# Pairing two tokens per partition, transposing them as one 32-bit element, and giving GpSimd half of an elementwise product

## The chip, the cores and the metric

The kernel runs on one NeuronCore of one Trainium2 chip. The metric is device time in microseconds (us); a figure for a kernel is the median of its runs. In this text PE is the TensorE matrix engine, PEld its weight loads, DVE the VectorE, ACT the ScalarE and POOL the GpSimd.

A program on one core still scatters: the kernel before ran between 224.1 and 230.8 us in all rounds of this study. Each comparison is therefore made with runs of the kernel before on the same chip in the same rounds. The record calls a run slow when it is more than 1.5% above the fastest run of the same kernel in those rounds, and the others fast. The medians here include slow runs, the ratios leave them out.

## The reference, cut to what matters

```python
def _attn_ref(x, f_logit, lower_bound):            # x, f_logit: (4, 6336, 256)
    sig = 1.0 / (1.0 + np.exp(-f_logit))
    f = lower_bound + (1.0 - lower_bound) * sig
    i = 1.0 - f
    for t in range(S):
        h = f[:, t] * h + i[:, t] * x[:, t]         # a scan over the tokens
        y[:, t] = h

def _moe_ref(x, w_h, w_t, b_t):                    # on the 25344 tokens of y
    H = np.maximum(x @ w_h, 0.0)
    T = 1.0 / (1.0 + np.exp(-(x @ w_t + b_t)))
    return T * H + (1.0 - T) * x
```

A recurrence over the tokens is followed by a small gated layer on each token.

## The kernel before

The tokens are cut into units of 1024 (a few are smaller, at the start and at the end). Tokens arrive on partitions, eight to a partition, and the scan runs along the free dimension (128x1024 in the profile), so PE transposes two intermediate values: `u` (the gate) and `bv` (gate times input).

```python
    def load(n, name, src):                        # token j*128 + p on partition p
        ...
            pin(nc.sync.dma_start(t[:, :nb], src[b, a:a + nb * P, :].rearrange("(j p) d -> p j d", p=P)))
    def gate(n):                                   # ACT: u = sigmoid(-f_logit), 16 bits
        ...
        pin(nc.scalar.activation(u[:np_, :nb], st[n]["lt"][:np_, :nb], AF.Sigmoid, scale=-1.0))
    def product(n, after):                         # POOL: bv = u * x, two tokens at a time
        ...
            ins = pin(nc.gpsimd.tensor_mul(bv[:np_, q:q + 2], st[n]["u"][:np_, q:q + 2], st[n]["xt"][:np_, q:q + 2]))
    def decay_pe(n, m):                            # PE: eight 16-bit transposes; b_pe does the same with bv
        ...
                pin(nc.tensor.transpose(uT[:, c + j * np_:c + (j + 1) * np_], st[n]["u"][:np_, j, h * P:(h + 1) * P],
                                        ident_h[:np_, :np_]))
```

After the transposes, ACT makes `f` from `uT`, and DVE scans (`y`). PE multiplies `y` with two weights (`gp`, `zp`), ACT makes `t` of `zp`, and DVE makes `d` of `gp`. The product `e = d * t` is shared: GpSimd takes the last `SHARE` of the 1024 columns, and it does so after DVE's part.

```python
    SHARE = 256

    def e_dve(n):
        N = width(n)
        e = ffn.tile([P, NH, NB * P], BF16, tag="e", name="e")
        ...
        ins = pin(nc.vector.tensor_mul(e[:, :, :M], d[:, :, :M], t[:, :, :M]))
        if M < N:
            follow(pin(nc.gpsimd.tensor_mul(e[:, :, M:N], d[:, :, M:N], t[:, :, M:N])), ins)
```

PE turns the result back to tokens in two halves. `o_pe(n, 0)` reads columns 0 to 511 of `e`, `o_pe(n, 1)` reads columns 512 to 1023, each with 8 matmuls on `y` and 8 on `e`, alternating; ACT copies the result `op` out as `o`.

```python
    def o_pe(n, q):
        ...
            for h in range(NH):
                o = op[:np_, j - j0, h * P:(h + 1) * P]
                pin(nc.tensor.matmul(o, st[n]["y"][:, h, cols], diag[:, h], start=True, stop=False))
                pin(nc.tensor.matmul(o, st[n]["e"][:, h, cols], ident_b, start=False, stop=True))
```

Of the kernel before, what the change touches and what calls it, by code (L numbers as in the profile page):

```python
# [11 lines left out]
FP32 = mybir.dt.float32  # L12
BF16 = mybir.dt.bfloat16
FP16 = mybir.dt.float16
AF = mybir.ActivationFunctionType
# [4 lines left out]
def kernel(  # L20
# [16 lines left out]
    nc = tc.nc  # L37
    B, S, D = x.shape
    assert D == 256
    P = 128  # L40
    NH = D // P
    NB = 8
# [5 lines left out]
    units = []  # L48
# [4 lines left out]
    for s0 in range(rest, S, NB * P):  # L53
        for b in range(B):
            last = s0 + NB * P == S and b == B - 1
            a = s0
# [5 lines left out]
    singles = ctx.enter_context(tc.tile_pool(name="singles", bufs=1))  # L62
    inp = ctx.enter_context(tc.tile_pool(name="inp", bufs=5))
    upool = ctx.enter_context(tc.tile_pool(name="upool", bufs=3))
    mid = ctx.enter_context(tc.tile_pool(name="mid", bufs=2))
# [5 lines left out]
    st = [dict() for _ in range(NU)]  # L71

    def pin(ins):
        return tc.keep_in_program_order(ins)

    def load(n, name, src):
        np_, nb, _, b, a = units[n]
        t = inp.tile([P, NB, D], FP32, tag=name, name=name)
        if isinstance(b, int):
            pin(nc.sync.dma_start(t[:, :nb], src[b, a:a + nb * P, :].rearrange("(j p) d -> p j d", p=P)))  # L80
        else:
            t4 = t[:np_, :nb].rearrange("p (b j) d -> p b j d", j=2)
            for j in range(2):
                pin(nc.sync.dma_start(t4[:, :, j], src[b, a + j * np_:a + (j + 1) * np_, :].rearrange("b p d -> p b d")))
        st[n][name] = t

    def store(n, j0, j1):
# [19 lines left out]
    for n in range(2):  # L107
        load(n, "lt", f_logit)
        load(n, "xt", x)

    ident_b = singles.tile([P, P], BF16, name="ident_b")
    make_identity(nc, ident_b)
    ident_h = singles.tile([P, P], FP16, name="ident_h")
    make_identity(nc, ident_h)

# [23 lines left out]

    def gate(n):  # L140
        np_, nb = units[n][:2]
        u = upool.tile([P, NB, D], FP16, tag="u")
        pin(nc.scalar.activation(u[:np_, :nb], st[n]["lt"][:np_, :nb], AF.Sigmoid, scale=-1.0))  # L143
        st[n]["u"] = u

    def follow(ins, after):

        if after is not None:
            tc.add_manual_dep(ins.ins, after.ins.name, mybir.DependencyInfo(
                mybir.DependencyClass.Sync, mybir.DependencyReason.DATA), reason="shared port")  # L150

    def product(n, after):
        np_, nb = units[n][:2]
        bv = mid.tile([P, NB, D], BF16, tag="bv")
        for q in range(0, nb, 2):
            ins = pin(nc.gpsimd.tensor_mul(bv[:np_, q:q + 2], st[n]["u"][:np_, q:q + 2], st[n]["xt"][:np_, q:q + 2]))  # L156
            if q == 0:
                follow(ins, after)
        st[n]["bv"] = bv

    def width(n):
        return units[n][0] * units[n][1]

    def both(n, m, key, make):


        if width(n) > 512:
            st[n][key, m] = make()
            yield st[n][key, m], m, 0
        elif m == 0:  # L170
            st[n][key, 0] = st[n][key, 1] = t = make()
            for k in range(NH):
                yield t, k, k * 512

    def col(n, m):
        return 0 if width(n) > 512 else m * 512

    def decay_pe(n, m):
        np_, nb = units[n][:2]
        for uT, h, c in both(n, m, "uT", lambda: ps1.tile([P, NB * P], FP16, tag="uT", name="uT")):  # L180
            for j in range(nb):
                pin(nc.tensor.transpose(uT[:, c + j * np_:c + (j + 1) * np_], st[n]["u"][:np_, j, h * P:(h + 1) * P],  # L182
                                        ident_h[:np_, :np_]))

    def decay_act(n, h):
        N, c = width(n), col(n, h)
# [3 lines left out]
                                 scale=ncc[:, h:h + 1], bias=1.0))  # L190

    def b_pe(n, m):
        np_, nb = units[n][:2]
        for bT, h, c in both(n, m, "bT", lambda: ps1.tile([P, NB * P], BF16, tag="bT", name="bT")):
            for j in range(nb):
                pin(nc.tensor.transpose(bT[:, c + j * np_:c + (j + 1) * np_], st[n]["bv"][:np_, j, h * P:(h + 1) * P],  # L196
                                        ident_b[:np_, :np_]))

    carry = {}

# [36 lines left out]
        pin(nc.vector.scalar_tensor_tensor(st[n]["d"][:, m, :N], st[n]["y"][:, m, :N], ncc[:, m:m + 1],  # L237
                                           st[n]["gp", m][:, c:c + N], op0=ALU.mult, op1=ALU.max))

    SHARE = 256  # L240

    def e_dve(n):

# [2 lines left out]
        st[n]["e"] = e  # L246
        M = N - SHARE if N == NB * P else N
        d, t = st[n]["d"], st[n]["t"]
# [33 lines left out]
    for n in range(-3, NU + 2):  # L282
        if ok(n + 4) and n + 4 > 1:
            load(n + 4, "lt", f_logit)
            load(n + 4, "xt", x)
        p, pp = n - 1, n - 2
# [11 lines left out]
        if ok(n + 1):  # L298
            decay_pe(n + 1, 0)
            decay_act(n + 1, 0)  # L300
        if ok(p):
            d_dve(p, 0)
        if ok(n):
            b_pe(n, 1)
# [10 lines left out]
        if ok(n + 2):  # L315
            gate(n + 2)
# [5 lines left out]
        if ok(n + 1):  # L322
            b_pe(n + 1, 0)
            decay_pe(n + 1, 1)
            decay_act(n + 1, 1)
# [4 lines left out]
        if ok(n + 2):  # L330
            product(n + 2, after)
# [32 lines left out]
```

## Time and profile before

| | kernel before |
|---|---|
| time, median of the first three runs | 226.26 us (226.25 to 229.24) |
| span of the profiled run | 226.9 us |
| start of POOL's first `e` of a full unit | 48.57 us |
| period of a unit (20 periods of POOL's `e`, 48.57 to 207.09) | 7.93 us |

The page's first part gives busy time and its share of the span:

```profile
PE 195.0 (86%) x2008; PEld 136.9 (60%) x2008; DVE 202.1 (89%) x159; ACT 199.1 (88%) x198; POOL 140.0 (62%) x131
```

Three engines stand close together, so a change that burdens one of them may change the bound.

The waits of the whole run (engine, line, what was waited for: us in total, times, longest) have few long ones:

```profile
DVE y L207 <- PE bT L196: 11.7, 5, 4.1
PE bT L196 <- DVE y L207: 8.3, 22, 2.5
```

DVE waited for PE's `bT` only five times, four of them before 44 us and one near the end (217.93 us), while PE waited for DVE 22 times. DVE sets the pace.

### The profile page before, as it was taken

Reading aid. Unit: us, or ns where it says so; the run is one execution under the profiler, and the core shown is the slowest. Engines: PE = TensorE matmul, PEld = TensorE weight load, DVE = VectorE, ACT = ScalarE, POOL = GpSimd, SP = SyncE. Lnnn points to the kernel's source line nnn. Section 1 sums busy time; section 2 is a strip of 40 time slices with the busy share of each in tenths; the row PEclk is TensorE's granted clock in tenths of the full one; section 3 lists DMA queues with packets and bytes.
Section 4 is the critical chain, followed back from the end, with each engine's and each line's share of the span. In section 5 each row is a group of like instructions: output and inputs, shape, how many; then the busy total and the mean of one; then the engine's idle time right before and its main releaser. Section 6 shows DMA issues by size and latency. Waiting matters only on the chain.

```text
span 226.9 us, 4999 instructions
## 1 busy us (share of the span) xinstructions
PE 195.0 (86%) x2008; PEld 136.9 (60%) x2008; DVE 202.1 (89%) x159; ACT 199.1 (88%) x198; POOL 140.0 (62%) x131
## 2 busy tenths in 40 slices
PE   0588495989999999999999999999999999998971
PEld 0356365656766666676666657666665766665661
DVE  1499657799999999999999999999999999999871
ACT  4459946799999999999999999999999999976873
POOL 2654870745966786696678669667866966764300
PEclk9999857899999999999999999999999999999998
DMA  6999999999999999999999999999999997542444
GB/s 179 307 386 386 383 390 390 390 390 387 399 385 385 399 394 389 384 397 382 382 391 395 388 390 402 395 384 403 396 387 397 396 349 276 202 185 95 185 185 185
DMA packets 60262, 78.69 MB, mean 347 GB/s; under 512 B 2384, under 2 KB 53584, under 8 KB 60240
## 3 DMA queue, kind: packets, MB, share of 16 engines
q1 hardware_dynamic: 59152, 77.86, 93.9%
q10 hardware_dynamic: 1088, 0.53, 0.9%
q8 instruction: 15, 0.25, 0.4%
q14 instruction: 7, 0.06, 0.1%
HBM read 52.43 MB, written 25.95 MB: 345 GB/s over the span
## 4 chain that ended last, share of the span: by engine, by line
DVE 52%; issue 23%; PE 13%; DMA 4%; ACT 3%; POOL 3%; DVEq 0%; SPq 0%; ACTq 0%; POOLq 0%
DVE y L207 25%; DVE d L237 19%; DVE e L249 8%; PE gp L218 4%; PE zp L218 3%; POOL bv L156 3%; DMA xt<-in_x_dram 2%; PE bT L196 2%; PE uT L182 2%; DMA lt<-in_f_logit_dram 1%; PE op L267 1%; PE op L268 1%; ACT o L276 1%; ACT u L143 1%; ACT t L231 1%
## 5 line engine op out<-in xcount | busy, mean ns | idle before, releaser
L156 POOL TENSOR_TENSOR bv<-u,xt 128x512 bf16<-128x512 f16 (+1 forms) x100 | 114.3, 1172 | 18.9 <-DMA xt<-in_x_dram 7.2
L207 DVE TENSOR_TENSOR_SCAN y<-f,y,bT 128x1024 bf16<-128x1024 f16 (+2 forms) x54 | 113.7, 2105 | 7.9 <-PE bT L196 7.6
L231 ACT ACTIVATE t<-zp,bt 128x1024 bf16<-128x1024 f32 (+3 forms) x58 | 56.9, 994 | 13.5 <-PE zp L218 13.5
L218 PEld LDWEIGHTS <-w_sb 128*128 128x128 f16 x408 | 39.7, 100 | 43.1 <-issue 10.0
L237 DVE SCALAR_TENSOR_TENSOR d<-y,ncc,gp 128x1024 bf16<-128x1024 bf16 (+3 forms) x58 | 63.8, 1101 | 1.0 <-PE gp L218 0.9
L189 ACT ACTIVATE f<-uT,ncc 128x1024 f16<-128x1024 f16 (+3 forms) x58 | 58.4, 1007 | 4.2 <-PE uT L182 4.2
L251 POOL TENSOR_TENSOR e<-d,t 128x512 bf16<-128x512 bf16 x22 | 25.5, 1159 | 56.3 <-PE gp L218 56.3
L218 PE MATMUL gp<-y,w_sb 128*128 128x512 bf16 (+2 forms) x204 | 53.3, 385 | 3.7 <-DVE d L237 1.3
L218 PE MATMUL zp<-y,w_sb 128*128 128x512 bf16 (+2 forms) x204 | 52.6, 382 | 0.1
L267 PE MATMUL op<-diag,y 128*128 128x128 f16 (+1 forms) x400 | 50.8, 221 | 2.2 <-ACT o L276 2.2
L276 ACT COPY o<-op 128x1024 f32<-128x1024 f32 (+2 forms) x51 | 50.9, 997 | 1.9 <-PE op L268 1.7
L143 ACT ACTIVATE u<-lt 128x2048 f16<-128x2048 f32 (+3 forms) x29 | 49.0, 1689 | 3.9 <-DMA lt<-in_f_logit_dram 3.9
L268 PE MATMUL op<-ident_b,e 128*128 128x128 bf16 (+1 forms) x400 | 50.8, 220 | 0.0
L268 PEld LDWEIGHTS <-e 128*128 128x128 bf16 (+1 forms) x400 | 44.9, 115 | 7.5 <-POOL bv L156 1.3
L267 PEld LDWEIGHTS <-y 128*128 128x128 bf16 (+1 forms) x400 | 45.0, 114 | 5.7 <-issue 0.3
L196 PE MATMUL bT<-ident_b,bv 128*128 128x128 bf16 (+1 forms) x400 | 32.8, 224 | 16.6 <-DVE y L207 8.3
L196 PEld LDWEIGHTS <-bv 128*128 128x128 bf16 (+1 forms) x400 | 26.9, 100 | 23.8 <-issue 15.2
L182 PE MATMUL uT<-ident_h,u 128*128 128x128 f16 (+1 forms) x400 | 32.4, 227 | 5.7 <-ACT u L143 5.7
L182 PEld LDWEIGHTS <-u 128*128 128x128 f16 (+1 forms) x400 | 26.1, 103 | 6.1 <-ACT u L143 5.7
L249 DVE TENSOR_TENSOR e<-d,t 128x1536 bf16<-128x1536 bf16 (+3 forms) x29 | 25.9, 892 | 3.6 <-ACT t L231 0.8
L207 DVE TENSOR_TENSOR_SCAN y<-f,bT 128x192 bf16<-128x192 f16 x8 | 3.9, 536 | 4.1 <-PE bT L196 4.1
L117 DVE TENSOR_SCALAR cc<-lb 128x2 f32<-128x2 f32 x1 | 0.2, 169 | 3.8 <-DMA lb<-in_lower_bound_dram 3.8
(16 smaller groups left out, 6.8 us busy)
## 6 DMA issues: line engine op xcount, KB each, us to landing
out_dram<-o SPq DMA_DIRECT2D x47, 512.0 KB, 7.2
lt<-in_f_logit_dram SPq DMA_DIRECT2D x22, 1024.0 KB, 9.4
xt<-in_x_dram SPq DMA_DIRECT2D x22, 1024.0 KB, 11.3
lt<-in_f_logit_dram SPq DMA_DIRECT2D x3, 512.0 KB, 7.6
xt<-in_x_dram SPq DMA_DIRECT2D x3, 512.0 KB, 6.7
lt<-in_f_logit_dram SPq DMA_DIRECT2D x4, 192.0 KB, 3.7
xt<-in_x_dram SPq DMA_DIRECT2D x4, 192.0 KB, 3.9
out_dram<-o SPq DMA_DIRECT2D x2, 384.0 KB, 9.3
```

The costliest lines, as they stand in the source:

```text
L143: pin(nc.scalar.activation(u[:np_, :nb], st[n]["lt"][:np_, :nb], AF.Sigmoid, scale=-1.0))
L156: ins = pin(nc.gpsimd.tensor_mul(bv[:np_, q:q + 2], st[n]["u"][:np_, q:q + 2], st[n]["xt"][:np_, q:q + 2]))
L182: pin(nc.tensor.transpose(uT[:, c + j * np_:c + (j + 1) * np_], st[n]["u"][:np_, j, h * P:(h + 1) * P], ident_h[:np_, :np_]))
L189: pin(nc.scalar.activation(st[n]["f"][:, h, :N], st[n]["uT", h][:, c:c + N], AF.Identity, scale=ncc[:, h:h + 1], bias=1.0))
L196: pin(nc.tensor.transpose(bT[:, c + j * np_:c + (j + 1) * np_], st[n]["bv"][:np_, j, h * P:(h + 1) * P], ident_b[:np_, :np_]))
L207: pin(nc.vector.tensor_tensor_scan(y[:, h, c0:c0 + ln], st[n]["f"][:, h, c0:c0 + ln], st[n]["bT", h][:, col(n, h) + c0:col(n, h) + c0 + ln ...
L218: pin(nc.tensor.matmul(p[:, c + a:c + e], w_sb[:, k, ki, h * P:(h + 1) * P], st[n]["y"][:, ki, a:e], start=ki == 0, stop=ki == NH - 1))
L231: pin(nc.scalar.activation(st[n]["t"][:, m, :N], st[n]["zp", m][:, c:c + N], AF.Sigmoid, bias=bt[:, m:m + 1]))
L237: pin(nc.vector.scalar_tensor_tensor(st[n]["d"][:, m, :N], st[n]["y"][:, m, :N], ncc[:, m:m + 1], st[n]["gp", m][:, c:c + N], op0=ALU.mult ...
L267: pin(nc.tensor.matmul(o, st[n]["y"][:, h, cols], diag[:, h], start=True, stop=False))
L268: pin(nc.tensor.matmul(o, st[n]["e"][:, h, cols], ident_b, start=False, stop=True))
L276: pin(nc.scalar.copy(st[n]["o"][:np_, j0:j1], st[n]["op"][:np_, :j1 - j0]))
```

## The change

The intent: two neighbouring tokens lie on one partition, so that a load reads runs of 2 KB instead of 1 KB. Their 16-bit `u` and `bv` values are stored side by side. PE then transposes each pair as one 32-bit element, which halves the number of transposes. DVE, the bound, gives another quarter of `e` to GpSimd.

```diff
     def load(n, name, src):
-            pin(nc.sync.dma_start(t[:, :nb], src[b, a:a + nb * P, :].rearrange("(j p) d -> p j d", p=P)))
+            pin(nc.sync.dma_start(pairs(t[:, :nb]), src[b, a:a + nb * P, :].rearrange("(k p j) d -> p k (j d)", p=P, j=2)))
     ...                                            (the short units likewise)
+    ident_f = singles.tile([P, P], FP32, name="ident_f")
+    make_identity(nc, ident_f)
     def gate(n):
-        u = upool.tile([P, NB, D], FP16, tag="u")
-        pin(nc.scalar.activation(u[:np_, :nb], st[n]["lt"][:np_, :nb], AF.Sigmoid, scale=-1.0))
+        u = upool.tile([P, NB // 2, D, 2], FP16, tag="u")
+        pin(nc.scalar.activation(inner(u[:np_, :nb // 2]), st[n]["lt"][:np_, :nb].rearrange("p (k j) d -> p k j d", j=2),
+                                 AF.Sigmoid, scale=-1.0))
     ...                                            (inner: "p k d j -> p k j d"; bv on GpSimd likewise)
+    def turn(n, t, key, h, c):
+        for k in range(nb // 2):
+            pin(nc.tensor.transpose(t[:, c + 2 * k * np_:c + 2 * (k + 1) * np_].bitcast(FP32),
+                                    st[n][key][:np_, k, h * P:(h + 1) * P].rearrange("p d j -> p (d j)").bitcast(FP32),
+                                    ident_f[:np_, :np_]))
     ...                                            (decay_pe and b_pe now call turn)
-    SHARE = 256
+    SHARE = 512
```

ACT thus walks through `u` in steps of two elements: the values of one token are written 4 bytes apart. GpSimd reads `u` and writes `bv` in the same steps. I call this the pair layout.

More of the change, by code (lines that the diff above doesn't have):

```diff
@@ L74, in pin, with pairs, inner @@
         return tc.keep_in_program_order(ins)
+    def pairs(t):
+        return t.rearrange("p (k j) d -> p k (j d)", j=2)
+    def inner(t):
+        return t.rearrange("p k d j -> p k j d")
     def load(n, name, src):
@@ L79, in load @@
         if isinstance(b, int):
-            pin(nc.sync.dma_start(t[:, :nb], src[b, a:a + nb * P, :].rearrange("(j p) d -> p j d", p=P)))
+            pin(nc.sync.dma_start(pairs(t[:, :nb]), src[b, a:a + nb * P, :].rearrange("(k p j) d -> p k (j d)", p=P, j=2)))
         else:
-            t4 = t[:np_, :nb].rearrange("p (b j) d -> p b j d", j=2)
-            for j in range(2):
-                pin(nc.sync.dma_start(t4[:, :, j], src[b, a + j * np_:a + (j + 1) * np_, :].rearrange("b p d -> p b d")))
+            pin(nc.sync.dma_start(pairs(t[:np_, :nb]), src[b, a:a + 2 * np_, :].rearrange("b (p j) d -> p b (j d)", j=2)))
         st[n][name] = t
@@ L153, in product @@
         np_, nb = units[n][:2]
-        bv = mid.tile([P, NB, D], BF16, tag="bv")
-        for q in range(0, nb, 2):
-            ins = pin(nc.gpsimd.tensor_mul(bv[:np_, q:q + 2], st[n]["u"][:np_, q:q + 2], st[n]["xt"][:np_, q:q + 2]))
-            if q == 0:
+        bv = mid.tile([P, NB // 2, D, 2], BF16, tag="bv")
+        for k in range(nb // 2):
+            ins = pin(nc.gpsimd.tensor_mul(inner(bv[:np_, k:k + 1])[:, 0], inner(st[n]["u"][:np_, k:k + 1])[:, 0],
+                                           st[n]["xt"][:np_, 2 * k:2 * k + 2]))
+            if k == 0:
                 follow(ins, after)
@@ L176, in col @@
         return 0 if width(n) > 512 else m * 512
+    def turn(n, t, key, h, c):
+        np_, nb = units[n][:2]
+        for k in range(nb // 2):
+            pin(nc.tensor.transpose(t[:, c + 2 * k * np_:c + 2 * (k + 1) * np_].bitcast(FP32),
+                                    st[n][key][:np_, k, h * P:(h + 1) * P].rearrange("p d j -> p (d j)").bitcast(FP32),
+                                    ident_f[:np_, :np_]))
     def decay_pe(n, m):
-        np_, nb = units[n][:2]
         for uT, h, c in both(n, m, "uT", lambda: ps1.tile([P, NB * P], FP16, tag="uT", name="uT")):
-            for j in range(nb):
-                pin(nc.tensor.transpose(uT[:, c + j * np_:c + (j + 1) * np_], st[n]["u"][:np_, j, h * P:(h + 1) * P],
-                                        ident_h[:np_, :np_]))
+            turn(n, uT, "u", h, c)
     def decay_act(n, h):
@@ L192, in b_pe @@
     def b_pe(n, m):
-        np_, nb = units[n][:2]
         for bT, h, c in both(n, m, "bT", lambda: ps1.tile([P, NB * P], BF16, tag="bT", name="bT")):
-            for j in range(nb):
-                pin(nc.tensor.transpose(bT[:, c + j * np_:c + (j + 1) * np_], st[n]["bv"][:np_, j, h * P:(h + 1) * P],
-                                        ident_b[:np_, :np_]))
+            turn(n, bT, "bv", h, c)
     carry = {}
```

## The prediction

> **What bounds the kernel now.** I read the page first: times by slice, the costliest groups, the chain that ended last. Then the table by stage, the groups with their shapes kept apart, the waits, and last the timeline of one period.
>
> In the table by stage the columns after the window are the busy time of PE, PEld, DVE, ACT and POOL, then PE's clock, the DMA share and GB/s.
>
> ```profile
> 30.00:40.00 10.00, 7.49 (x57) 5.38 (x56) 6.30 (x6) 6.00 (x7) 3.71 (x4) 0.67 1.08 390
> 120.00:140.00 20.00, 19.07 (x204) 13.38 (x202) 19.79 (x13) 19.50 (x19) 15.48 (x14) 1.00 1.07 394
> 190.00:200.00 10.00, 9.50 (x93) 6.34 (x93) 9.79 (x8) 8.89 (x10) 6.50 (x6) 1.00 0.61 220
> ```
>
> There is a start of some 45 us with holes, then a steady state in which DVE, ACT and PE are all busy over 95%, and an end. DMA moves about 390 GB/s until the loads run out near 190 us; the engines keep their pace when it falls to 220, so transfers do not set the steady pace. The chain in order of time shows who does:
>
> ```profile
> 123.14 2.34 DVE y L207
> 125.48 1.18 DVE d L237
> 126.76 0.96 DVE e L249
> 127.79 2.10 issue
> 129.89 0.80 DVE d L237
> 130.70 0.37 issue
> 131.07 2.34 DVE y L207
> ```
>
> From one y to the second next is one unit of 1024 tokens: 131.07 - 123.14 = 7.93 us, all of it DVE ("issue" here is the other scan and the rest of d). There are 22 such units, so 22 x 7.93 = 174 us of the 227 are this period. ACT is close behind: the starts of its seven instructions of a period, where it does not wait, add up to about 7.6 us.
>
> The rows the change touches, by shape (busy us, mean ns):
>
> ```profile
> L156 POOL TENSOR_TENSOR bv<-u,xt 128x512 bf16<-128x512 f16 x96 | 109.6, 1171 | 13.0 <-DVE e L249 6.3 <-ACT u L143 4.9 <-DMA xt<-in_x_dram 1.3
> L251 POOL TENSOR_TENSOR e<-d,t 128x512 bf16<-128x512 bf16 x22 | 25.5, 1159 | 56.3 <-PE gp L218 56.3
> L249 DVE TENSOR_TENSOR e<-d,t 128x1536 bf16<-128x1536 bf16 x22 | 21.1, 958 | 2.3
> L182 PE MATMUL uT<-ident_h,u 128*128 128x128 f16 x384 | 30.8, 225 | 0.0
> ```
>
> POOL has room: 4 x 1.17 + 1.16 = 5.8 us of 7.93. Its 56.3 us of idle time before e is in fact a wait for DVE's e, since the text orders it after that.
>
> The timeline shows how the engines interlock within a period:
>
> ```profile
> 127.86 1.16 POOL L251 TENSOR_TENSOR e<-d,t 128x512 bf16<-128x512 bf16 x1 [2.26 <-PE gp L218]
> 128.43 0.22 PE L267 MATMUL op<-diag,y 128*128 128x128 f16 x1
> 129.32 0.61 PE L182 MATMUL uT<-ident_h,u 128*128 128x128 f16 x8
> 130.03 0.61 PE L196 MATMUL bT<-ident_b,bv 128*128 128x128 bf16 x8
> 131.07 2.34 DVE L207 TENSOR_TENSOR_SCAN y<-f,y,bT 128x1024 bf16<-128x1024 f16 x1
> ```
>
> After DVE's e (126.76) PE starts the first half of op at 128.43, then transposes uT, then bT, and the scan at 131.07 reads this bT. The bT transposes end at 130.64, so their slack to the scan is 0.43 us. PE reached them at about 129.76 and waited until 130.03 for the scan before to free the buffer: another 0.27. PE may thus be about 0.7 us late in op before DVE notices.
>
> [...] In this trace the 16-bit transposes start every 55 ns[...]. A 32-bit transpose no row shows. [...]
>
> **The change part by part.** *Load runs of 2 KB.* [...] Of the waits only six are for loads, 11 us together and nearly all before 14 us[...].
>
> *Transposes.* 32 of 16 bits per unit become 16 of 32 bits. [...] A block of 8 took 8 x 55 = 0.45 us; a block of 4 takes 0.22 us at 55 ns each[...]. I take about 110 ns: the same block time as before, PE's sum unchanged.
>
> *The strided writes of u and bv.* [...] I expect no change.
>
> *Half of e on GpSimd.* DVE's e shrinks from 128x1536 to 128x1024: 0.96 to 0.69 us, which is what the one such e of the start took when POOL was idle. Alone this would be 0.27 x 22 = 6 us off the DVE. POOL's e doubles: 2 x 1.16 = 2.3 us; its sum per unit becomes 4.7 + 2.3 = 7.0 us, which still fits.
>
> *A wait that moves.* The built program tells what the diff does not. Before, PE waited for POOL's share of e only at the first e load of the second half of op, most of a period later. Now this wait stands in the first half, at its fourth matmul (the second load of e): with the larger share the dependency tracker takes the two regions to overlap, although the first half's columns are all DVE's. This closes a loop. From the start of DVE's e to the start of the next:
> - DVE e 0.69; handover to POOL 0.14 (127.72 to 127.86); POOL e 2.30; handover 0.06: 3.19
> - the remaining 13 of 16 op matmuls, 0.0555 each: 0.72
> - uT block 0.45; bT block to the start of the scan 0.71 (0.61 and 0.10, as once at 43.19 to 43.90): 1.16
> - scan and d up to the next e: 126.76 - 123.14 = 3.62
>
> The sum is 8.69 us, against 7.93 - 0.27 = 7.66 for DVE alone. So DVE waits about 1 us per unit for bT, and the period grows by 0.76 us. Times 22 it is 16.7 us. [...] Small handovers may be counted too long, so I say 241.
>
> **The rivals.** *A: it gets faster.* If the moved wait cost nothing, DVE's period would be 7.66 and ACT's 7.6 to 7.8, for 22 x 0.15 to 0.27 = 3 to 6 us[...]: 220 to 223. For it: DVE bounds the period and loses work[...]. Against it: POOL's e ends 3.1 us after DVE's e began, while PE comes to op after 1.67, and only 0.7 us of slack is there, of which the shorter e takes 0.27.
> *B: transposes at full speed.* With 55 ns each, two blocks in the loop save 2 x 0.23: 8.23[...]. With some slack misjudged it would come out as the same.
> *C: transposes are slow.* [...]
> *D: strided GpSimd.* If bv slows by half, POOL needs 2.3 + 4 x 1.75 = 9.3 and with DVE's e before it about 10 us per unit: over 270. [...]
> *E: the start.* PE's clock fell to 0.5 twice between 26 and 41 us, after PE had waited there. [...]
>
> **Range and chances.** The lower edge is B with a lucky start, 230; the upper is C, 262. Faster needs the loop under 7.7 us, that is transposes at no cost at all: 5%. Within 2% (up to 230.8) means B with some gain at the start: 15%. Slower is the rest, 80%.
>
> **What would show it.** Right: DVE's scan y idles for PE bT some 0.8 to 1 us in each unit; PE (or its weight load) waits in op for POOL's e, 22 times about 1 us; POOL's e of 128x1024 takes 2.3 us, DVE's 0.69, bv still 1.17; y of one unit to y of the next 8.5 to 8.9 us[...]. [...] Wrong: no wait of PE for POOL in op and a period below 7.9 (A); a spacing of the transposes near 55[...]; a POOL row for bv above 1.3 us (D); or a start that differs by more than 3 us (E).

In full, the sum of the forecast came to 242 us: 226.3, plus 16.7 for the periods, less 0.7 for faster loads at the start; from that I said 241. The term of 0.7 is cut, since the load rate behind it was an assumption of mine. Cut with it are the sum of B (232, the same 0.7 taken off), the whole of C (its sum gave the upper edge of 262) and what E allowed for the start (3 us either way). The 110 ns of a 32-bit transpose, twice the 55 measured for a 16-bit one, and the unchanged `u` and `bv` stay as assumptions: the trace before shows none of the three.

## More of the kernel before

ACT's timeline in one unit (start, duration, engine, line) shows how to measure an engine whose records overlap: take the time from one start to the next.

```profile
124.68 1.93 ACT L143 ACTIVATE u<-lt 128x2048 f16<-128x2048 f32 x1
126.48 1.03 ACT L276 COPY o<-op 128x1024 f32<-128x1024 f32 x1
```

The record of `u` has 1.93 us, but the next instruction starts after 126.48 - 124.68 = 1.80.

## The result, and the profile after

The changed kernel is correct and **slower: 246.59 us** (243.92 to 247.0, 4 runs) against 226.33 us (226.25 to 229.24, 4 runs) for the kernel before. The ratio is 1.084, with a 95% interval of 1.072 to 1.095. Ratios here are the mean time of one kernel's fast runs over that of the other's fast runs of the same rounds, so they are not quite the ratio of the medians.

In the page's first part the shares of PE and DVE fell, from 86 and 89% to 81 and 82% of a longer span:

```profile
PE 198.7 (81%) x1608; PEld 134.9 (55%) x1608; DVE 200.2 (82%) x159; ACT 213.4 (87%) x198; POOL 173.1 (71%) x133
```

These shares average over the start and the end. In the table by stage (columns as explained in the prediction) the first two of the stages shown there now read:

```profile
30.00:40.00 10.00, 7.44 (x38) 4.76 (x38) 4.68 (x4) 6.47 (x7) 7.26 (x6) 0.66 1.05 407
120.00:140.00 20.00, 17.37 (x142) 11.44 (x140) 18.12 (x12) 19.56 (x18) 16.18 (x11) 1.00 1.02 366
```

PE and DVE lost their density in the steady stage (19.07 and 19.79 before). DVE no longer sets the pace alone. ACT kept it at 19.56, which will matter later. The chain that ended last, followed through one period (start, us, what), names the loop:

```profile
128.61 0.70 DVE e L261
129.35 0.08 issue
129.45 2.13 POOL e L263
131.59 0.05 issue
131.63 0.25 PE op L280
...
132.55 0.44 PE uT L192 x4
132.99 0.45 PE bT L192 x4
133.44 0.03 issue
133.49 0.04 issue
133.54 2.35 DVE y L219
135.88 1.18 DVE d L249
137.06 0.03 issue
137.11 0.04 issue
137.16 0.70 DVE e L261
```

From `e` to `e` is 137.16 - 128.61 = 8.55 us. The chain goes from DVE to POOL, to PE and back to DVE. Before, it stayed on DVE. In PE's timeline the first three matmuls of this half of `op` start at 130.40, 130.45 and 130.50, and the fourth, the second that reads `e`, only at 131.63, when POOL is done. The waits say the same:

```profile
DVE y L219 <- PE bT L192: 28.1, 25, 4.0
PEld L280 <- POOL e L263: 23.6, 22, 1.2
PE op L280 <- POOL e L263: 20.2, 22, 1.0
```

The wait of PE for POOL's `e` occurs once in each of the 22 units, and DVE waits for `bT` 25 times instead of five. In the steady state each of these waits of DVE is 0.80 us. The rows of the changed operations by shape (busy us, mean ns of one, then idle before):

```profile
L165 POOL TENSOR_TENSOR bv<-u,xt 128x512 bf16<-128x512 f16 x96 | 120.7, 1292 | 16.1 <-DVE e L261 5.8 <-PE gp L230 5.0 <-PE op L280 3.3
L263 POOL TENSOR_TENSOR e<-d,t 128x1024 bf16<-128x1024 bf16 x22 | 46.8, 2125 | 39.6 <-DVE e L261 39.6
L151 ACT ACTIVATE u<-lt 128x2048 f16<-128x2048 f32 x22 | 55.6, 2528 | 0.0
```

The elementwise work of the pair layout is not free: `bv` takes 1.29 us instead of 1.17, and ACT's `u` 2.53 instead of 1.93.

Where did the time go? By the starts of POOL's `e`, the first is at 52.60 us instead of 48.57, the 21st at 223.43 instead of 207.09. So the start cost 4.0 us more, 20 periods cost 20 x (8.54 - 7.93) = 12.3 us more, and the rest of the span 2.0 us more (245.2 - 223.43 against 226.9 - 207.09). The sum, 18.3 us, is the difference of the two spans. The profiled run of the kernel before took 229.0 us, 2.7 above its median, and that of the changed kernel 247.0, 0.4 above its own, which is why the medians differ by two more (20.3).

### The profile page after: what moved, and what is told of

Read it like the earlier page. It is cut to its first block, busy times and chain, and to the rows that moved or that the text cites. A ratio compares the mean times of both kernels' runs of the same rounds, so it can differ in the third digit from the quotient of the medians.

```text
span 245.2 us, 4221 instructions
## 1 busy us (share of the span) xinstructions
PE 198.7 (81%) x1608; PEld 134.9 (55%) x1608; DVE 200.2 (82%) x159; ACT 213.4 (87%) x198; POOL 173.1 (71%) x133
## 4 chain that ended last, share of the span: by engine, by line
DVE 38%; PE 23%; POOL 22%; DMA 7%; issue 4%; ACT 3%; DVEq 0%; POOLq 0%; SPq 0%; ACTq 0%
DVE y L219 21%; POOL e L263 18%; DVE d L249 10%; DVE e L261 6%; PE op L280 6%; PE bT L192 5%; PE uT L192 5%; POOL bv L165 4%; DMA lt<-in_f_logit_dram 4%; PE op L279 4%; DMA w_raw<-in_moe_w_h_dram 3%; PE zp L230 2%; PE gp L230 2%; ACT o L288 1%; ACT u L151 1%
## 5 line engine op out<-in xcount | busy, mean ns | idle before, releaser
L165 POOL TENSOR_TENSOR bv<-u,xt 128x512 bf16<-128x512 f16 (+1 forms) x100 | 125.7, 1291 | 20.7 <-DVE e L261 5.8
L263 POOL TENSOR_TENSOR e<-d,t 128x1024 bf16<-128x1024 bf16 x22 | 46.8, 2125 | 39.6 <-DVE e L261 39.6
L280 PE MATMUL op<-ident_b,e 128*128 128x128 bf16 (+1 forms) x400 | 53.7, 222 | 20.2 <-POOL e L263 20.2
L151 ACT ACTIVATE u<-lt 128x2048 f16<-128x2048 f32 (+3 forms) x29 | 64.0, 2206 | 2.3 <-DMA lt<-in_f_logit_dram 2.2
L280 PEld LDWEIGHTS <-e 128*128 128x128 bf16 (+1 forms) x400 | 44.5, 114 | 31.3 <-POOL e L263 23.6
L279 PE MATMUL op<-diag,y 128*128 128x128 f16 (+1 forms) x400 | 53.1, 220 | 1.8 <-ACT o L288 1.8
L192 PE MATMUL bT<-ident_f,bv 128*128 128x128 f32 (+1 forms) x200 | 37.8, 294 | 10.9 <-DVE y L219 5.7
L192 PE MATMUL uT<-ident_f,u 128*128 128x128 f32 (+1 forms) x200 | 32.3, 287 | 6.8 <-ACT u L151 6.2
L192 PEld LDWEIGHTS bT<-ident_f,bv 128*128 128x128 f32 (+1 forms) x200 | 23.9, 147 | 20.2 <-POOL bv L165 13.7
L192 PEld LDWEIGHTS uT<-ident_f,u 128*128 128x128 f32 (+1 forms) x200 | 23.7, 149 | 7.3 <-issue 6.4
L261 DVE TENSOR_TENSOR e<-d,t 128x1024 bf16<-128x1024 bf16 (+2 forms) x29 | 21.1, 727 | 3.4 <-ACT t L243 0.4
```

Source lines behind the costliest of these rows:

```text
L151: pin(nc.scalar.activation(inner(u[:np_, :nb // 2]), st[n]["lt"][:np_, :nb].rearrange("p (k j) d -> p k j d", j=2), AF.Sigmoid, scale=-1.0))
L165: ins = pin(nc.gpsimd.tensor_mul(inner(bv[:np_, k:k + 1])[:, 0], inner(st[n]["u"][:np_, k:k + 1])[:, 0], st[n]["xt"][:np_, 2 * k:2 * k + 2]))
L192: pin(nc.tensor.transpose(t[:, c + 2 * k * np_:c + 2 * (k + 1) * np_].bitcast(FP32), st[n][key][:np_, k, h * P:(h + 1) * P].rearrange("p d ...
```

## The experiments

My theory: the larger share moves PE's wait for POOL's `e` from the second half of `op` into the first half, and this closes the loop; the other parts of the change cost little. Rivals: the pair layout (32-bit transposes, 4-byte steps) costs the time, or the loads and the start do. Twelve runs followed; two of them are of the same kernel. "Period" is always the mean of 20 periods of POOL's `e`.

### after_share256: the changed kernel without the larger share

```diff
-    SHARE = 512
+    SHARE = 256
```

> The changed kernel with GpSimd's share of e back at a quarter; the 32-bit transposes and 2 KB loads stay. Theory (the moved wait of PE for POOL's e closes the loop): the wait is gone from the first half of op, the period falls from 8.55 us to what ACT needs with the slower u, 7.6 + 0.6 = 8.2 us, so about 20 x 0.33 = 6.5 us less than the changed kernel, near 240 us; DVE waits on ACT or PE in another place. Rival (the new layout and its transposes cost the time, the share costs nothing): the period stays at 8.5 us and the time at 245 to 247 us.

Measured: correct, 234.02 us (232.99 to 234.45), ratio to before 1.033 (1.024 to 1.041). That is 6 us below the 240 that I expected: in the profiles 8.5 us come from the 20 periods, 2.0 from the start and 2.1 from the end. The period is 8.12 us. PE's wait for POOL's `e` is gone from the list of waits, so the larger share is what put it there. But the time did not fall to that of the kernel before. ACT's timeline, without any idle time between its instructions, shows why:

```profile
120.58 2.85 ACT L151 ACTIVATE u<-lt 128x2048 f16<-128x2048 f32 x1
122.95 1.33 ACT L288 COPY o<-op 128x1024 f32<-128x1024 f32 x1
123.84 1.46 ACT L204 ACTIVATE f<-uT,ncc 128x1024 f16<-128x1024 f16 x1
```

From `u` to the next start is 2.37 us, 0.57 more than before. (All records of ACT are longer here than when it has pauses, 1.46 us for `f` against 1.12 to 1.15, but their starts are as far apart as ever, 1.00. The longer records by themselves cost nothing here.) From one `u` to the next is 8.15 us: ACT alone now sets the pace. A second, independent cost lay under the wait.

### before_share512: the kernel before with only the larger share

```diff
-    SHARE = 256
+    SHARE = 512
```

> The kernel before with only the share of e raised to a half; 16-bit transposes, 1 KB loads. Theory: the wait moves here too, PE waits about 1 us for POOL's e in each unit, the period becomes 8.4 to 8.6 us: 226.3 + 20 x 0.6 = about 238 us; POOL's e takes 2.1 us, u stays at 1.93 and bv at 1.17 us. Rival (layout and transposes cost the time): 220 to 226 us, because DVE only loses work.

Measured: correct, 241.47 us (239.11 to 244.66), ratio 1.063 (1.050 to 1.075), some 3 us above the 238 that I expected. The period is 8.55 us, the same as with the whole change. The waits:

```profile
PEld L268 <- POOL e L251: 25.6, 22, 1.2
DVE y L207 <- PE bT L196: 25.1, 24, 4.7
```

With 16-bit transposes, 1 KB loads and the old layout, the same 22 waits come back, and the period with them. The larger share is sufficient for the slow steady state. The pair layout adds nothing to the period while the loop binds.

### after_split and before_split512: e in two tiles

The columns that the first half of `op` reads are all DVE's. Only the tracking of dependencies within one tile makes PE wait for POOL there. With a tile for each engine's part, the wait should go and every true dependency stay. (Why the tracking finds an overlap at 512 columns and not at 256 is not shown.)

```diff
-        e = ffn.tile([P, NH, NB * P], BF16, tag="e", name="e")
+        e = ffn.tile([P, NH, NB * P - SHARE], BF16, tag="e", name="e")
 ...
-            follow(pin(nc.gpsimd.tensor_mul(e[:, :, M:N], d[:, :, M:N], t[:, :, M:N])), ins)
+            e2 = ffn.tile([P, NH, SHARE], BF16, tag="e2", name="e2")
+            st[n]["e2"] = e2
+            follow(pin(nc.gpsimd.tensor_mul(e2, d[:, :, M:N], t[:, :, M:N])), ins)
 ...
+            e = st[n]["e2" if q else "e"]
-                pin(nc.tensor.matmul(o, st[n]["e"][:, h, cols], ident_b, start=False, stop=True))
+                pin(nc.tensor.matmul(o, e[:, h, ecols], ident_b, start=False, stop=True))
```

(`ecols` are the same columns, counted from the start of the half. In before_split512 `SHARE` is 512 too.)

> The changed kernel with e kept in two tiles, one written by DVE and one by GpSimd, so that the first half of op waits for DVE alone; the arithmetic is the same. Theory: PE's wait for POOL's e in the first half of op disappears with the share still at a half; the period falls to ACT's 8.2 to 8.3 us and the time to about 240 us. If only the moved wait and nothing else was the cause, it would fall to 7.7 us and some 228 us. Rival (a longer POOL e slows the others by itself): nothing changes, 246 us.

> The kernel before with the share at a half and e in two tiles: the part of the change that takes work off DVE, without the moved wait and without the new layout. Theory: the period falls from 7.93 to about 7.7 us (DVE 7.66, ACT 7.6): 226.3 - 20 x 0.23 = about 221.5 us, faster by 2%. Rival (POOL's sum of 6.7 us per unit delays bv[...]): 226 us or more, with DVE or PE waiting for POOL bv.

Measured: after_split is correct, 234.52 us (234.05 to 235.97), ratio 1.037 (1.026 to 1.047), period 8.14. PE's wait for POOL's `e` is gone, and the chain that ended last runs on ACT, here over a whole unit:

```profile
121.27 2.40 ACT u L151
123.67 0.86 ACT o L292
...
126.13 1.32 ACT o L292
127.45 1.02 ACT f L204
128.46 1.00 ACT t L243
129.47 2.40 ACT u L151
```

From `u` to `u` is 129.47 - 121.27 = 8.20 us. This is the same floor as in after_share256, reached by the other way. Freed of the moved wait, the changed kernel falls by 12 us (the ratio from 1.084 to 1.037), to less than the 240 that I expected, and then stands on ACT.

before_split512 is correct, **222.41 us** (221.58 to 223.58), ratio 0.982 (0.974 to 0.991), period 7.75. This beats both kernels: the larger share does pay once the wait is out of the way. What it then waits for:

```profile
PE bT L196 <- POOL bv L156: 14.2, 25, 1.3
```

POOL, with `e` of 2.13 us and four `bv` of 1.17, now holds back PE. The periods alternate: one takes 7.66 us, DVE's own work without a pause, and the next 7.84, in which DVE waits for the late `bT`. The chain that ended last goes through POOL's `bv` as well, so a still larger share should not help (not run).

### after_contig and after_split_contig: ACT writes u in memory order

To find which side of ACT's `u` costs, ACT writes the pairs contiguously and instead reads the logits alternately from the two tokens.

```diff
-        pin(nc.scalar.activation(inner(u[:np_, :nb // 2]), st[n]["lt"][:np_, :nb].rearrange("p (k j) d -> p k j d", j=2),
+        pin(nc.scalar.activation(u[:np_, :nb // 2], st[n]["lt"][:np_, :nb].rearrange("p (k j) d -> p k d j", j=2),
```

> The changed kernel with one line of the gate turned: ScalarE walks u in the order in which it lies (pairs adjacent, writes unbroken) and lt with a step of one token; the result is the same. Theory (writing 2-byte elements at a 4-byte step is what lengthened u from 1.93 to 2.53 us): u takes 1.93 us again. Because the moved wait still closes the loop at 8.55 us, the time stays within 1% of the changed kernel, 243 to 247 us. Rival (the four-dimensional walk itself costs, or strided reads cost as much): u stays at 2.5 us or more.

> Both obstacles taken away from the changed kernel: e in two tiles, and u written unbroken; 32-bit transposes, 2 KB loads and the half share stay. Theory (moved wait and slower ACT are the two bounds): ACT falls to 7.6 us per unit, the period to 7.7 to 7.9 us (DVE 7.66, or PE waiting for POOL's bv at 1.29 us each), the time to 222 to 227 us, against 234.5 with the split alone. Rival (the 32-bit transposes cost PE time of their own): the period stays above 8 us with PE busy throughout, 230 us or more.

Measured: after_contig is correct, one look of 244.17 us (its state is unknown, so I read only its durations and its period). Its row:

```profile
L151 ACT ACTIVATE u<-lt 128x2048 f16<-128x2048 f32 x22 | 52.8, 2399 | 0.0
```

`u` takes 2.40 us, not 1.93. This expectation missed: a read that jumps from token to token (1 KB apart) costs 0.47 us for 2048 elements, nearly as much as a write in 4-byte steps, 0.60. The period stayed at 8.54, so a shorter `u` gains nothing while the loop binds.

after_split_contig is correct, 232.5 us (231.11 to 233.25), ratio 1.019 (1.010 to 1.027), with a period of 8.06. I had hoped for 222 to 227. ACT still has no idle time, with `u` 2.27 us from start to start. The cost moved from the write to the read, and most of it stayed.

### after_split_plainu and after_split_plain: the pair layout's elementwise cost by itself

In the first, ACT writes and reads `u` plainly. In the second, GpSimd's `bv` is plain too. Both have `e` in two tiles and keep the 2 KB loads and the 32-bit transposes.

```diff
-        pin(nc.scalar.activation(inner(u[:np_, :nb // 2]), st[n]["lt"][:np_, :nb].rearrange("p (k j) d -> p k j d", j=2),
+        pin(nc.scalar.activation(u[:np_, :nb // 2].rearrange("p k d j -> p k (d j)"), pairs(st[n]["lt"][:np_, :nb]),
 (the second also:)
-            ins = pin(nc.gpsimd.tensor_mul(inner(bv[:np_, k:k + 1])[:, 0], inner(st[n]["u"][:np_, k:k + 1])[:, 0],
-                                           st[n]["xt"][:np_, 2 * k:2 * k + 2]))
+            ins = pin(nc.gpsimd.tensor_mul(bv[:np_, k].rearrange("p d j -> p (d j)"),
+                                           st[n]["u"][:np_, k].rearrange("p d j -> p (d j)"),
+                                           st[n]["xt"][:np_, 2 * k:2 * k + 2].rearrange("p j d -> p (j d)")))
```

> The changed kernel with e in two tiles, and ScalarE writing u plainly (neighbouring elements, no 4-byte steps), so that the result is wrong on purpose. Theory (the 4-byte-step output of ScalarE's u is what ScalarE pays for the pair layout, and with the moved wait gone ScalarE sets the period): u 128x2048 back at 1.93 us, start to start 1.80 as in the kernel before, ScalarE's unit about 7.6 us, so it has idle time again; the period falls from 8.20 to 7.75 to 7.95 (now TensorE waiting for GpSimd's bv, which still writes in steps of 4 bytes and takes 1.29), the time from 234.5 to 225 to 230 us. Rival (u is slow for another reason, say GpSimd working beside it): u stays at 2.5, the period at 8.2 and the time at 234.

> As the run before, and GpSimd's bv read and written plainly too (wrong on purpose). What is then left of the change against the kernel before with 512 columns and two tiles of e (222.4 us, period 7.74) are the 2 KB load runs and the 32-bit transposes. Theory: bv 1.17 us, period 7.74, time 222 to 226 us: the 32-bit transposes cost TensorE nothing on the chain. Rival (32-bit transposes or the load order cost something that the traces hide): period 7.85 or more, time over 227.

Measured: after_split_plainu took 229.62 us (227.3 to 230.19), ratio 1.007 (1.000 to 1.014). Its period of 7.98 is just above the range that I gave. `u` is back at its old length, beside everything else that the change brought:

```profile
L151 ACT ACTIVATE u<-lt 128x2048 f16<-128x2048 f32 x22 | 42.5, 1931 | 0.0
L165 POOL TENSOR_TENSOR bv<-u,xt 128x512 bf16<-128x512 f16 x96 | 120.2, 1285 | 10.5 <-DVE e L261 3.5 <-PE zp L230 3.5 <-ACT u L151 2.3
```

So the access pattern is what makes `u` slow, not what works beside it. ACT has idle time again, and PE now waits for POOL's `bv`, still 1.29 us. after_split_plain took 225.0 us (224.31 to 225.39), ratio 0.988 (0.982 to 0.994), with `bv` at 1.175 us and a period of 7.76. (Whether `bv` loses its 0.12 us by the read or by the write in steps is not separated.) The period is that of before_split512 (7.75), although 2 KB loads and 32-bit transposes are in: these two add nothing to the period where DVE and POOL's `bv` bind.

### before_2kb: the kernel before with only the 2 KB load runs

The result is wrong on purpose (the tokens are not in the order that the rest expects). That wrong values leave the times as they are is my assumption, here and in the two runs above.

```diff
-            pin(nc.sync.dma_start(t[:, :nb], src[b, a:a + nb * P, :].rearrange("(j p) d -> p j d", p=P)))
+            pin(nc.sync.dma_start(t[:, :nb].rearrange("p (k j) d -> p k (j d)", j=2), src[b, a:a + nb * P, :].rearrange("(k p j) d -> p k (j d)", p=P, j=2)))
```

> The kernel before with the load runs alone changed to 2 KB (tokens are then in the wrong order, so the result is wrong on purpose[...]). Theory (loads are hidden after the start): GB/s in the early slices rises from 386 to about 405, the period stays at 7.93 us, the time within 1% of the kernel before, plus or minus 2 us from the start. Rival (the 1 KB runs held the steady state back): 222 us or less.

Measured: 229.45 us (227.03 to 231.17) against 227.81 in the same rounds, ratio 1.003 (0.993 to 1.012): the same. The table by stage, this kernel:

```profile
10.00:20.00 10.00, 7.28 (x63) 4.42 (x61) 8.99 (x17) 5.46 (x9) 4.68 (x5) 1.00 1.06 403
```

The loads run at 403 GB/s instead of 385 in this stage, and the period of 7.93 does not move. The transfers were hidden before, and making them faster gained nothing. The second weight arrived later: 7.2 us after its request against 5.8 in the kernel before. DVE waited for it, as it did in the changed kernel (start, duration, and in brackets the idle time):

```profile
12.64 0.49 DVE L142 TENSOR_SCALAR w_sb<-w_raw,cc 128x512 f16<-128x512 f32 x1 [0.78 <-DMA w_raw<-in_moe_w_h_dram]
```

### after_split_w and before_split512_w: the weights requested first

Is the late weight what the start lost? Both kernels have `e` in two tiles and the three requests moved ahead of the first loads.

```diff
     nc.scalar.dma_start(lb, lower_bound.rearrange("(h p) -> p h", p=P))
+    load_weights()
     for n in range(2):
         load(n, "lt", f_logit)
 ...
-        if n + 2 == 0:
-            load_weights()
```

> The changed kernel with e in two tiles, and the weights asked for before the first loads instead of after the first gate. It asks where the 2 to 4 us at the start went. Theory (the loads are queued sooner and the weights land behind them, so the scan of the second unit starts at 16.2 instead of 13.2 us): that scan starts near 13.5 us, POOL's first e some 2 us sooner than 50.1, and the time falls from 234.5 to about 232.5 us. Rival (the start is bound by the gate and the clock of PE, not by the weights): the first e comes no sooner, since the loads themselves now land some 1.4 us later, and the time stays.

> The kernel before with 512 columns on GpSimd, e in two tiles, and the weights requested ahead of the first loads. If the late weights hold back the start: 0.5 to 1.5 us off 222.4. If not (as in the changed kernel with early weights, where nothing was gained): 222.4 within 0.7.

(The 1.4 us in the expectation of after_split_w are what 512 KB of weights take at the 386 GB/s of the page before, an estimate. In the trace of that run the second `u` starts at 9.09 us, after 1.17 us of waiting for its load; in the changed kernel it starts at 7.84 without a wait.)

Measured: after_split_w is correct, 234.03 us (233.2 to 238.39), against 234.52 without the edit in other rounds. The first scan of the second unit starts at 15.33 us instead of 16.19, but POOL's first `e` at 49.66 instead of 50.08. Of the 2 us that I expected, 0.4 came: the late weight is not what holds most of the start.

before_split512_w is correct, 226.95 us (225.55 to 229.22), ratio 0.995 (0.988 to 1.002). Against before_split512, which ran in other rounds on another chip, that is some 4 us **worse** by the medians and 3 by the ratios, which neither expectation had. Its period is the same 7.75. In the profiles the whole difference is in the start, where POOL's first `e` is at 49.59 instead of 44.39, 5.2 us later. Of these, 2.8 are there by the first scan of a full unit (31.67 instead of 28.91): the very first scan starts 1.6 us later (11.31 instead of 9.68), with the weights' transfers ahead of its loads, and DVE's four weight operations take longer. The other 2.4 us are lost in the stage after that. In the table by stage (first before_split512, then before_split512_w):

```profile
30.00:40.00 10.00, 7.49 (x95) 5.86 (x94) 8.92 (x7) 8.41 (x9) 6.54 (x7) 1.00 1.08 390
```

```profile
30.00:40.00 10.00, 6.79 (x51) 4.47 (x51) 5.13 (x4) 6.70 (x7) 5.64 (x5) 0.68 1.08 390
```

PE's granted clock was 0.68 in this stage instead of 1.00. I looked at it in all profiles: where it was 1.00 (three runs), POOL's first `e` came at 44.11 to 45.99 us; at 0.83 to 0.86 (four runs) at 45.95 to 49.55; at 0.66 to 0.69 (seven runs, the kernels before and after among them) at 48.57 to 52.60. A low clock goes with a late start. Most of these kernels differ in other ways too, but two pairs do not. before_split512 and its repeat (next section) are one program: they start the first scan of a full unit at 28.91 and 28.80 us, have the clock at 1.00 and 0.86, and reach POOL's first `e` at 44.39 and 45.95. The kernel before and before_share512 do the same work up to the first full `e`. They start that scan at 28.65 and 28.64, but the clock is 0.67 in the one (its line is in the prediction) and 1.00 in the other:

```profile
30.00:40.00 10.00, 7.49 (x95) 5.81 (x93) 8.92 (x8) 8.41 (x10) 6.57 (x6) 1.00 1.08 390
```

Their first `e` comes at 48.57 and 44.11, and only 0.27 of these 4.5 us are DVE's shorter `e`. In the kernel before, PE is busy all the time from 32 to 34 us at a clock of 0.50, while DVE does nothing and waits 3.45 us for `bT`. The dip thus goes with 1.6 to 4.2 us, between programs that are equal up to there. What sets it off is open.

### before_split512_again

Since the start varies so, the best kernel ran once more with five rounds.

> The kernel before with 512 columns of e on GpSimd and e in two tiles, once more and with five rounds, since the same kernel with early weights kept the period of 7.75 us but lost 4.5 us at the start. If the first result holds, 221.5 to 224 us and a ratio of 0.975 to 0.99 to the kernel before, first e of GpSimd at 44 to 46 us. If the low value came from a lucky start, about 226 us and a ratio of 0.99 to 1.0, first e near 48.

Measured: 223.32 us (222.33 to 224.23, 6 runs) against 226.82 (224.09 to 229.79, 11 runs), ratio 0.987 (0.981 to 0.992), period 7.75, with PE's clock at 0.86 between 30 and 40 us and the first `e` at 45.95. The gain is real, and it is smaller than 2%.

### The steady state in one table

| kernel | share | `e` | layout | period, us | what binds |
|---|---|---|---|---|---|
| before | 256 | one tile | plain | 7.93 | DVE |
| before_share512 | 512 | one tile | plain | 8.55 | loop with POOL's `e` |
| after | 512 | one tile | pairs | 8.54 | the same loop |
| after_share256 | 256 | one tile | pairs | 8.12 | ACT |
| after_split | 512 | two tiles | pairs | 8.14 | ACT |
| after_split_plainu | 512 | two tiles | `u` plain | 7.98 | POOL's `bv` |
| after_split_plain | 512 | two tiles | `u`, `bv` plain | 7.76 | DVE, and POOL's `bv` in every second unit |
| before_split512 | 512 | two tiles | plain | 7.75 | DVE, and POOL's `bv` in every second unit |

The costs do not add up; the longest one shows. With the wait in place, the slower `u` is invisible; with either one mended alone, the other remains.

## Why the prediction was right or wrong

**The verdict and the range were right:** slower, 246.6 us within 230 to 262, with the centre at 241 set 5.6 us too low.

**The bound and the moved wait were right.** The loop came out as 8.55 us against 8.69. By its terms: DVE's `e` and handover 0.84 (predicted 0.83); POOL's `e` 2.13 (2.30, since twice the columns cost less than 2 x 1.16); handover 0.05 (0.06); the rest of `op` 0.92 (0.72, as the first matmul after the wait shows 0.25 on the chain and I had counted it as 0.055); `uT` 0.44 (0.45); `bT` to the scan 0.55 (0.71); scan and `d` 3.62 (3.62). before_share512 shows that the share alone makes this loop, and after_split that two tiles take it away.

**The 32-bit transposes were right.** A block of four takes 0.44 to 0.45 us, 110 ns each from start to start, as I had assumed, against 55 for a 16-bit one; this disposes of rival B, which had 55, and of C, which had them slower still. after_split_plain, with a period of 7.76 against 7.75, shows that the steady state does not feel them.

**The 2 KB loads: they came faster, and were worth nothing.** In the stages from 10 to 40 us the changed kernel moved 403 to 408 GB/s and the kernel before 384 to 390, but the 0.7 us at the start did not come.

**"I expect no change", of the strided writes, was the step that failed outright.** The reason that I gave for `u` is shown by no run. `u` went from 1.93 to 2.53 us. It did not spoil the time only because the loop, at 8.55, is longer than ACT's unit, and that was luck. That unit I had read as about 7.6; with 0.6 more it is 8.2. It did spoil rival A: without the wait the time would not be 220 to 223 but 234.5, as after_split shows. And `bv`, expected at 1.17 us, took 1.29. That was just under the limit of 1.3 that I had set for rival D, and it costs 0.21 us of the period as soon as POOL binds (after_split_plainu against after_split_plain).

**The sizes.** I predicted 22 x 0.76 = 16.7 us for the steady part. A period grew by 0.62, there are 20 of them, and they cost 12.3 us; with 2.0 in the end that is 14.3. I predicted -0.7 for the start, and it cost +4.0. The start is the term that was mis-sized most, and it even has the wrong sign.

The early part of it belongs to the loads and the layout. The first scan of a full unit starts at 28.6 to 28.9 us in the profiles with the old layout and 1 KB loads and the weights requested in their old place (four), at 29.6 with the 2 KB loads alone, at 30.5 and 31.3 in the two runs with plain access, and at 32.1 to 32.9 in those with the pair layout (five, the weights likewise in their old place). In the profile of the changed kernel 2.9 of the 4.3 us are there by the second unit's first scan (16.11 instead of 13.17): the very first scan starts 1.0 us later, DVE comes to the late weight 0.9 later, and the four weight operations take 1.1 longer. before_2kb has 0.7, 0.9 and nothing of these. In the traces of both kernels and of the runs before_2kb, before_split512 and both with early weights, each weight operation of more than 1 us (1.12 to 1.49) lies beside a `bv` of POOL, and those that ran with POOL idle took 0.5 us or less. That POOL's work is what stretches them was not tested. The dip of PE's clock does not explain the 4.0 us, since the kernels before and after both have it (0.67 and 0.66). It goes with differences between single runs (rival E's limit was 3 us, the equal programs above show 1.6 to 4.2), and why it comes in some and not in others is open.

## What to carry to other kernels

Before a share of work is moved to another engine, ask who will wait for it earlier than before: here the same share cost 0.62 us per period with the wait in place (before_share512, 8.55 against 7.93) and gained 0.18 without it (before_split512, 7.75). Look in the built program at which instruction waits for which, above all where two engines write parts of one tile, and give each writer its own tile. When a layout saves instructions on one engine, price the strided accesses that it puts on the others: here 0.57 us from start to start for each `u` on ACT (2.37 against 1.80) and 0.12 for each `bv` on POOL. And when a wait is removed, compute the next floor first: after_split fell from 8.54 to 8.14 and stood on ACT.
